# Interleaving the two projections with clustered attention, under one activation table set

## The chip, the cores and the metric

The kernel runs on one core of a Trainium2 chip. The metric is the device time of one execution in microseconds (us). A core has a matrix engine (TensorE, PE in the profile, with its weight loads as PEld), a vector engine (VectorE, DVE), an engine for activation functions (ScalarE, ACT), a general one (GpSimd, POOL) and an engine that here only issues transfers (SyncE, SP). Each works through its own queue in order and waits for others at semaphores.

## The reference

Attention over 4 batches, 8 heads, 768 positions of 64 values, in which a query sees only the keys of its own cluster, and then two projections with a gelu between them:

```python
q_assign = np.argmax(np.einsum('bhsd,hcd->bhsc', q_n, c_n), axis=-1)
k_assign = np.argmax(np.einsum('bhsd,hcd->bhsc', k_n, c_n), axis=-1)
mask = q_assign[:, :, :, None] == k_assign[:, :, None, :]
scores = np.where(mask, scale * np.matmul(q, k.transpose(0, 1, 3, 2)), -1000000000.0)
attn = softmax(scores)                       # over the keys
attn_out = np.matmul(attn, v)                # [4, 8, 768, 64]
x = attn_out.transpose(0, 2, 1, 3).reshape(3072, 512)
out = gelu(x @ w_in) @ w_out                 # w_in [512, 2048], w_out [2048, 512]
```

There are 16 cluster centroids per head. The function returns float32 [3072, 512].

## The kernel before, in words

Two stages follow each other.

The attention stage runs over 32 heads (4 batches of 8). The loop over `t` (line 260) is a software pipeline written out by hand: while head `t` has its scores, exps and value products, head `t+1` gets its one-hot cluster rows and head `t+2` its transposes and cluster dots. The 768 positions are 6 chunks of 128.

- Preparing a head: q and k are split into a bf16 part and its remainder (lines 128 to 132, VectorE), transposed on TensorE (line 152), copied to `q_stack` and `k_stack` (line 156), multiplied with the centroids (line 163), reduced to one-hot rows of the nearest centroid (lines 171 to 180, VectorE), which are transposed too (line 187) and copied under the 64 data rows (lines 192 and 194). So one product of 80 rows gives the score plus a large bonus where the clusters agree.
- Scores: for each key chunk a tile `e_ps` of 128 keys by 768 queries (line 202, as 512 and 256 columns; two such tiles in PSUM). ScalarE takes its exp with scale and bias into `e_sb` (line 211).
- Value products: `v_sb` of a chunk carries 64 columns of values and 64 of ones, so the product with `e_sb` (line 219) gives numerators in rows 0 to 63 of `av_ps` and the sum of exps in rows 64 to 127. `av_ps` is one tile of 768 columns, accumulated over the 6 chunks.
- Closing a head: VectorE copies the numerators (line 229), ScalarE takes the logarithm of the denominators straight from `av_ps` (line 230), then exp(-log) as the reciprocal (line 237), and VectorE writes their product to `xT` in bf16 (line 240).

The projection stage runs over 6 blocks of 512 tokens: 16 tiles of `x @ w_in` (line 333, 4 matmuls of 512 columns each, four PSUM tiles), each followed by a gelu (line 338), and then 4 output tiles (line 343, 16 matmuls of 512 columns each, four PSUM tiles), copied by VectorE and ScalarE in turn (lines 350 and 352) and stored (line 359).

In the code, the transposes and dots of head `t+2` are "fills", handed out between the chunks by `emit_fills`. Tile pools say how many buffers each tile has, and a scheduler sets the final order of each engine's queue from the program order and the dependences. The activation functions come from table sets; a load is put in wherever the next function isn't in the set that is active.

Of the kernel before, what the change touches and what calls it, by code (L numbers as in the profile page):

```python
# [18 lines left out]
def kernel(  # L19
# [22 lines left out]
    SCALE = 1.0 / float(D) ** 0.5  # L42
    SPLITS = [(0, 512), (512, 256)]
# [11 lines left out]
    cent_sq = consts.tile([H * NCL, 1], FP32)  # L55
    cent_scr = consts.tile([H * NCL, D], FP32)
    nc.scalar.activation(cent_scr, cent_sb, ACT.Square, accum_out=cent_sq)
    cent_norm = consts.tile([H * NCL, 1], FP32)
    nc.scalar.sqrt(cent_norm, cent_sq)
    cent_rnorm = consts.tile([H * NCL, 1], FP32)  # L60
    nc.vector.reciprocal(cent_rnorm, cent_norm)
    cent_n = consts.tile([H * NCL, D], FP32)
# [3 lines left out]
    with tc.tile_pool(name="ps_init", bufs=1, space=bass.MemoryType.PSUM) as ps_init:  # L66
# [6 lines left out]
            out=cn_big[0:D, :, :, 1],  # L73
# [4 lines left out]
    w_in_sb = consts.tile([P, DM // P, DF], BF16)  # L78
    w_out_sb = consts.tile([P, DF // P, DM], BF16)
# [14 lines left out]
    xT = xt_pool.tile([P, DM // P, NTOK], BF16)  # L94

    NIT = B * H
    NV = 4

    with tc.tile_pool(name="qk", bufs=3) as qk_pool, \
# [3 lines left out]
         tc.tile_pool(name="rcp", bufs=2) as rcp_pool, \  # L103
         tc.tile_pool(name="ps_stk", bufs=1, space=bass.MemoryType.PSUM) as ps_stk_pool, \
         tc.tile_pool(name="ps_e", bufs=2, space=bass.MemoryType.PSUM) as ps_e_pool, \
         tc.tile_pool(name="ps_av", bufs=1, space=bass.MemoryType.PSUM) as ps_av_pool:

        st = {}

        def st_dma_qk(i):  # L110
            b, h = divmod(i, H)
            s = st.setdefault(i, {})
            s["q_sb"] = qk_pool.tile([P, NCH, D], FP32, name="q_sb")
            s["k_sb"] = qk_pool.tile([P, NCH, D], FP32, name="k_sb")
            nc.sync.dma_start(out=s["q_sb"], in_=q[b, h].rearrange("(p x) d -> p x d", p=P))
            nc.sync.dma_start(out=s["k_sb"], in_=k[b, h].rearrange("(p x) d -> p x d", p=P))

        def st_dma_v(i):
            b, h = divmod(i, H)
            nc.gpsimd.dma_start(  # L120
                out=v_sb[:, i % NV, :, 0:D],
                in_=v[b, h].rearrange("(p x) d -> p x d", p=P))
# [85 lines left out]

        def st_exp(i, j):
            s = st[i]  # L210
            nc.scalar.activation(s["e_sb"][:, j, :], s["e_ps_j"], ACT.Exp,  # L211
                                 bias=ebias, scale=SCALE)

        def st_av(i, j):
            s = st[i]
            if j == 0:
                s["av_ps"] = ps_av_pool.tile([P, S], FP32, name="av_ps")
            for (c0, cw) in SPLITS:
                nc.tensor.matmul(  # L219
                    s["av_ps"][:, c0:c0 + cw],  # L220
                    v_sb[:, i % NV, j, :],
                    s["e_sb"][:, j, c0:c0 + cw],
                    start=(j == 0), stop=(j == NCH - 1))

        def st_avrelease(i):
            s = st[i]
            num = rcp_pool.tile([D, S], FP32, name="num")
            lnden = rcp_pool.tile([D, S], FP32, name="lnden")
            nc.vector.tensor_copy(num, s["av_ps"][0:D, :])  # L229
            nc.scalar.activation(lnden, s["av_ps"][D:2 * D, :], ACT.Ln)  # L230
            s["num"], s["lnden"] = num, lnden

        def st_norm(i):
            b, h = divmod(i, H)
            s = st[i]
            recip = rcp_pool.tile([D, S], FP32, name="recip")
            nc.scalar.activation(recip, s["lnden"], ACT.Exp, scale=-1.0)  # L237
            col = (h % 2) * D
            chunk = h // 2
            nc.vector.tensor_tensor(  # L240
                out=xT[col:col + D, chunk, b * S:(b + 1) * S],
                in0=s["num"], in1=recip, op=ALU.mult)
            del st[i]

        st_dma_qk(0), st_dma_qk(1), st_dma_qk(2)
        st_dma_v(0), st_dma_v(1)
# [13 lines left out]
        for t in range(NIT):  # L260
            if t + 3 < NIT:
                st_dma_qk(t + 3)
            if t + 2 < NIT:
                st_dma_v(t + 2)
            if t + 2 < NIT:
                st_hilo(t + 2)

            st_qk(t, 0)
            st_exp(t, 0)
            st_qk(t, 1)  # L270
            st_exp(t, 1)

            if t + 1 < NIT:
                st_ohT(t + 1)
                st_scatter(t + 1)

            p2 = t + 2 < NIT
            if p2:
                st_alloc_ps(t + 2)

            fills = []
            if p2:
                fills += [("T", "q", j) for j in range(NCH)]
                fills += [("SC", "q", None)]
                fills += [("T", "k", j) for j in range(NCH)]
                fills += [("SC", "k", None)]
                fills += [("D", "q", j) for j in range(NCH)]
                fills += [("D", "k", j) for j in range(NCH)]
            per_chunk = [0, 2, 6, 8, 10, 10]

            fi = 0

            def emit_fills(n):
                nonlocal fi
                cnt = 0
                while fi < len(fills) and cnt < n:
                    kind, side, j = fills[fi]
                    if kind == "T":
                        st_transpose(t + 2, side, j)
                    elif kind == "SC":  # L300
                        st_stackcopy(t + 2, side)
                        cnt -= 1
                    else:
                        st_dots(t + 2, side, j)
                    fi += 1
                    cnt += 1

            for j in range(NCH):
                emit_fills(per_chunk[j])
                st_av(t, j)  # L310
                if j + 2 < NCH:
                    st_qk(t, j + 2)
                    st_exp(t, j + 2)
            st_avrelease(t)
            emit_fills(10 ** 9)
            if p2:
                st_rowmax(t + 2)
            st_norm(t)

    TOKB = 512  # L320
    NTB = NTOK // TOKB

    with tc.tile_pool(name="moe_g", bufs=2) as moe_pool, \
         tc.tile_pool(name="moe_out", bufs=4) as out_pool, \
         tc.tile_pool(name="ps_h", bufs=4, space=bass.MemoryType.PSUM) as psum_h, \
         tc.tile_pool(name="ps_o", bufs=4, space=bass.MemoryType.PSUM) as psum_o:

        for tb in range(NTB):
            g_sb = moe_pool.tile([P, DF // P, TOKB], BF16, name="g_sb")
            for ft in range(DF // P):  # L330
                h_ps = psum_h.tile([P, TOKB], FP32, name="h_ps")
                for c in range(DM // P):
                    nc.tensor.matmul(  # L333
                        h_ps,
                        w_in_sb[:, c, ft * P:(ft + 1) * P],
                        xT[:, c, tb * TOKB:(tb + 1) * TOKB],
                        start=(c == 0), stop=(c == DM // P - 1))
                nc.scalar.activation(g_sb[:, ft, :], h_ps, ACT.Gelu)  # L338

            for tt in range(TOKB // P):  # L340
                o_ps = psum_o.tile([P, DM], FP32, name="o_ps")
                for ft in range(DF // P):
                    nc.tensor.matmul(  # L343
                        o_ps,
                        g_sb[:, ft, tt * P:(tt + 1) * P],
                        w_out_sb[:, ft, :],
                        start=(ft == 0), stop=(ft == DF // P - 1))
                o_sb = out_pool.tile([P, DM], FP32, name="o_sb")
                if tt % 2 == 0:
                    nc.vector.tensor_copy(o_sb, o_ps)  # L350
                else:
                    nc.scalar.copy(o_sb, o_ps)  # L352
                g0 = tb * TOKB + tt * P
                bb = g0 // S
                c0 = g0 % S
                x = c0 // P
                dst = out[bb * S:(bb + 1) * S].rearrange(
                    "(p x) m -> x p m", x=NCH)[x]
                nc.sync.dma_start(out=dst, in_=o_sb)


# [28 lines left out]
```

The softmax here doesn't subtract the row's maximum and nothing guards it: scores larger than these inputs give would overflow.

## Time and profile before

The median of five runs is 548.79 us (547.28 to 550.07); the profiled execution spans 547.0 us.

| group of the page | count | busy us | mean ns of one |
|---|---|---|---|
| exp of a score tile, line 211 (ACT) | 192 | 168.5 | 896 |
| table loads at lines 211 and 230 (ACT) | 64 | 82.2 | 1283 |
| logarithm, line 230, and reciprocal, line 237 (ACT) | 64 | 52.4 | 807, 830 |
| scores, line 202 (PE) | 384 | 122.9 | 399 |
| value products, line 219 (PE) | 384 | 120.8 | 413 |
| projections, lines 333 and 343 (PE) | 768 | 171.4 | 388, 379 |
| copy of the numerators, line 229 (DVE) | 32 | 30.3 | 948 |
| product with the reciprocal, line 240 (DVE) | 32 | 30.4 | 951 |

How to read it: busy time is the union of a group's executions, while the mean is of one execution with its latency. Matmuls overlap one another, so their busy time over their count is the price of one in a stream, and less than the mean. The page also shows TensorE's granted clock in tenths of full speed, in 40 slices of the span. A group's last column is the idle time of its engine just before it, with what ended most of that.

### The profile page before, as it was taken

What the parts mean: (1) busy time and instruction counts of PE and PEld (TensorE: products, weight loads), DVE (VectorE), ACT (ScalarE), POOL (GpSimd) and SP (SyncE); (2) the same over time, 40 slices, a digit from 0 to 9 for tenths busy, and PEclk for the clock granted to TensorE, in tenths of its full rate; (3) what the DMA queues carried; (4) which work ended last, traced back from release to release, by engine and by line L of the source; (5) the groups of instructions that cost most, each with busy time, mean ns of one, the idle gap of its engine ahead of it and who ended that gap; (6) DMA issues with size and microseconds to landing.
All of it is one profiled execution on the core that took longest, in us unless ns stands there. A gap on an engine that the chain in (4) does not pass through costs nothing.

```text
span 547.0 us, 6319 instructions
## 1 busy us (share of the span) xinstructions
PE 429.1 (78%) x2497; PEld 221.6 (41%) x2497; DVE 231.6 (42%) x532; ACT 369.0 (67%) x437; POOL 38.9 (7%) x63
## 2 busy tenths in 40 slices
PE   0367867977776777777677677677999999999997
PEld 0244433443443444344444343332444444444443
DVE  3675665565666666566656767421000000000000
ACT  2038898898889888888888999987434342425250
POOL 4330100100010010001000100000000000000000
PEclk9997797676788787778868989858899999999999
DMA  8992231232123223222322311000020102020201
GB/s 191 252 170 36 34 60 24 40 41 50 23 52 43 38 36 50 46 37 36 59 50 38 53 13 8 1 0 1 0 78 6 72 0 78 0 78 0 78 0 77
DMA packets 40813, 26.65 MB, mean 49 GB/s; under 512 B 26960, under 2 KB 37200, under 8 KB 40784
## 3 DMA queue, kind: packets, MB, share of 16 engines
q0 software_dynamic: 27968, 7.34, 13.4%
q1 hardware_dynamic: 12816, 18.91, 10.9%
q8 instruction: 19, 0.31, 0.2%
q14 instruction: 10, 0.08, 0.1%
HBM read 27.30 MB, written 6.29 MB: 61 GB/s over the span
## 4 chain that ended last, share of the span: by engine, by line
PE 55%; ACT 38%; DMA 3%; DVE 2%; issue 1%; SPq 0%; ACTq 0%
ACT e_sb L211 16%; PE h_ps L333 15%; PE o_ps L343 15%; PE av_ps L219 11%; PE e_ps L202 9%; ACT L230 8%; ACT L211 7%; ACT lnden L230 5%; DMA k_sb<-in_k_dram 3%; PE q_ps L152 2%; ACT recip L237 1%; PE k_ps L152 1%; PE q_ps L187 1%; ACT L338 1%; PE q_ps L163 1%
## 5 line engine op out<-in xcount | busy, mean ns | idle before, releaser
L211 ACT ACTIVATE e_sb<-e_ps,ebias 128x768 bf16<-128x768 f32 x192 | 168.5, 896 | 45.4 <-PE e_ps L202 42.1
L219 PE MATMUL av_ps<-e_sb,v_sb 128*128 128x512 bf16 (+1 forms) x384 | 120.8, 413 | 72.8 <-ACT lnden L230 38.5
L202 PE MATMUL e_ps<-q_stack,k_stack 80*128 80x512 bf16 (+1 forms) x384 | 122.9, 399 | 10.5 <-ACT e_sb L211 9.2
L333 PE MATMUL h_ps<-xT,w_in_sb 128*128 128x512 bf16 x384 | 87.2, 388 | 3.1 <-ACT g_sb L338 3.1
L343 PE MATMUL o_ps<-w_out_sb,g_sb 128*128 128x512 bf16 x384 | 84.2, 379 | 0.3 <-ACT lnden L230 0.3
L219 PEld LDWEIGHTS <-v_sb 128*128 128x128 bf16 x384 | 40.4, 111 | 99.8 <-issue 90.8
L338 ACT ACTIVATE g_sb<-h_ps 128x512 bf16<-128x512 f32 x96 | 56.9, 598 | 25.1 <-PE h_ps L333 25.0
L350 DVE COPY o_sb<-o_ps 128x512 f32<-128x512 f32 x12 | 8.3, 692 | 150.7 <-PE o_ps L343 150.7
L240 DVE TENSOR_TENSOR xT<-num,recip 64x768 bf16<-64x768 f32 x32 | 30.4, 951 | 87.2 <-ACT recip L237 87.2
L202 PEld LDWEIGHTS <-k_stack 80*128 80x128 bf16 x384 | 43.2, 116 | 43.9 <-issue 30.1
L333 PEld LDWEIGHTS <-w_in_sb 128*128 128x128 bf16 x384 | 38.3, 100 | 51.1 <-issue 7.8
L211 ACT ACT_TABLE_LOAD x32 | 41.1, 1283 | 24.9 <-PE e_ps L202 24.3
L352 ACT COPY o_sb<-o_ps 128x512 f32<-128x512 f32 x12 | 7.0, 586 | 74.3 <-PE o_ps L343 74.3
L343 PEld LDWEIGHTS <-g_sb 128*128 128x128 bf16 x384 | 37.6, 98 | 45.7 <-issue 0.6
L120 POOL DMA_DIRECT2D v_sb<-in_v_dram x32 | 26.2, 820 | 275.8 <-PE av_ps L219 255.9
L230 ACT ACT_TABLE_LOAD x32 | 41.1, 1283 | 0.6
L229 DVE COPY num<-av_ps 64x768 f32<-64x768 f32 x32 | 30.3, 948 | 17.9 <-PE av_ps L219 17.2
L152 PE MATMUL q_ps<-ident,q_hl 128*128 128x128 bf16 x192 | 24.7, 280 | 11.1 <-DVE cn_big L72 9.9
L152 PEld LDWEIGHTS <-q_hl 128*128 128x128 bf16 x192 | 19.5, 129 | 23.4 <-DVE cn_big L72 10.2
L152 PE MATMUL k_ps<-ident,k_hl 128*128 128x128 bf16 x192 | 26.5, 253 | 2.2 <-DVE dsum L172 2.2
L237 ACT ACTIVATE recip<-lnden 64x768 f32<-64x768 f32 x32 | 26.6, 830 | 0.0
L230 ACT ACTIVATE lnden<-av_ps 64x768 f32<-64x768 f32 x32 | 25.8, 807 | 0.4
(51 smaller groups left out, 305.1 us busy)
## 6 DMA issues: line engine op xcount, KB each, us to landing
q_sb<-in_q_dram SPq DMA_DIRECT2D x32, 192.0 KB, 2.4
k_sb<-in_k_dram SPq DMA_DIRECT2D x32, 192.0 KB, 2.4
out_dram<-o_sb SPq DMA_DIRECT2D x24, 256.0 KB, 2.0
v_sb<-in_v_dram POOLq DMA_DIRECT2D x32, 96.0 KB, 3.0
w_in_sb<-in_moe_w_in_dram POOLq DMA_DIRECT2D x4, 512.0 KB, 11.6
w_out_sb<-in_moe_w_out_dram POOLq DMA_DIRECT2D x16, 128.0 KB, 8.2
cent_sb<-in_centroids_dram SPq DMA_DIRECT2D x1, 32.0 KB, 1.8
```

The costliest lines, as they stand in the source:

```text
L120: nc.gpsimd.dma_start(out=v_sb[:, i % NV, :, 0:D], in_=v[b, h].rearrange("(p x) d -> p x d", p=P))
L152: nc.tensor.transpose(ps[:, j * P:(j + 1) * P], hl[:, j, :], ident)
L202: nc.tensor.matmul(e_ps[:, c0:c0 + cw], s["k_stack"][0:AUG, j * P:(j + 1) * P], s["q_stack"][0:AUG, c0:c0 + cw], start=True, stop=True)
L211: nc.scalar.activation(s["e_sb"][:, j, :], s["e_ps_j"], ACT.Exp, bias=ebias, scale=SCALE)
L219: nc.tensor.matmul(s["av_ps"][:, c0:c0 + cw], v_sb[:, i % NV, j, :], s["e_sb"][:, j, c0:c0 + cw], start=(j == 0), stop=(j == NCH - 1))
L229: nc.vector.tensor_copy(num, s["av_ps"][0:D, :])
L230: nc.scalar.activation(lnden, s["av_ps"][D:2 * D, :], ACT.Ln)
L237: nc.scalar.activation(recip, s["lnden"], ACT.Exp, scale=-1.0)
L240: nc.vector.tensor_tensor(out=xT[col:col + D, chunk, b * S:(b + 1) * S], in0=s["num"], in1=recip, op=ALU.mult)
L333: nc.tensor.matmul(h_ps, w_in_sb[:, c, ft * P:(ft + 1) * P], xT[:, c, tb * TOKB:(tb + 1) * TOKB], start=(c == 0), stop=(c == DM // P - 1))
L338: nc.scalar.activation(g_sb[:, ft, :], h_ps, ACT.Gelu)
L343: nc.tensor.matmul(o_ps, g_sb[:, ft, tt * P:(tt + 1) * P], w_out_sb[:, ft, :], start=(ft == 0), stop=(ft == DF // P - 1))
```

## The change

It has three parts that depend on each other.

1. One table set for exp and logarithm. A load of the set numbered 6, which holds both, is put into ScalarE's queue by hand: once after the square root of the setup, and again after the gelus of each projection block but the last. Exps are ordered after it without a semaphore, and the gelus after the last reciprocal before them.
2. PSUM room. The value products go through one bank of 512 columns in two passes: columns 0 to 511 along with the chunks as before, then 512 to 767 for all six chunks at once. VectorE copies numerators and denominators together to `nd` in SBUF after each pass, and ScalarE takes the logarithm from there. The bank that this frees holds an output tile of the down-projection (one buffer).
3. Projections inside the loop over heads. A batch's up-projection and gelus are called as one block, one head after the batch's last (after the last head, for the last batch), in tiles of 768 columns that use the score tiles' buffers. Its down-projection is cut into single matmuls and handed out between the chunks of the following heads: 2 after each chunk, 3 and 2 around the second pass. What is left goes before the next block, and after the loop for the last batch.

It is for taking most table loads off ScalarE, and for giving TensorE projection work while it would wait in the attention stage.

The diff, cut to its core:

```diff
+        load_ln_exp([sqrt_inst])
...
-                s["av_ps"] = ps_av_pool.tile([P, S], FP32, name="av_ps")
-            for (c0, cw) in SPLITS:
-                nc.tensor.matmul(
-                    s["av_ps"][:, c0:c0 + cw],
+                s["av_ps"] = ps_av_pool.tile([P, 512], FP32, name="av_ps")
+            nc.tensor.matmul(
+                s["av_ps"][:, 0:cw],
...
-            nc.vector.tensor_copy(num, s["av_ps"][0:D, :])
-            nc.scalar.activation(lnden, s["av_ps"][D:2 * D, :], ACT.Ln)
+            nc.vector.tensor_copy(s["nd"][:, c0:c0 + cw], s["av_ps"][:, 0:cw])
+            if pss == 1:
+                s["lnden"] = rcp_pool.tile([D, S], FP32, name="lnden")
+                nc.scalar.activation(s["lnden"], s["nd"][D:2 * D, :], ACT.Ln)
...
+        def emit_m1_block(bb):
+            g_sb = g_pool.tile([P, DF // P, S], BF16, name="g_sb")
+            for ft in range(DF // P):
+                h_ps = ps_e_pool.tile([P, S], FP32, name="e_ps")
+                for (c0, cw) in SPLITS:
+                    for c in range(DM // P):
+                        nc.tensor.matmul(
+                            h_ps[:, c0:c0 + cw],
+                            w_in_sb[:, c, ft * P:(ft + 1) * P],
+                            xT[:, c, bb * S + c0:bb * S + c0 + cw],
+                            start=(c == 0), stop=(c == DM // P - 1))
+                gelus.append(nc.scalar.activation(g_sb[:, ft, :], h_ps, ACT.Gelu))
+            for g in gelus:
+                after_inst(g, last_recip[0])
+            if bb < B - 1:
+                load_ln_exp(gelus)
...
+        def emit_m2(bb, x):
+            o_ps = ps_moe_pool.tile([P, DM], FP32, name="o_ps")
+            for ft in range(DF // P):
+                nc.tensor.matmul(
+                    o_ps, g_sb[:, ft, x * P:(x + 1) * P], w_out_sb[:, ft, :],
+                    start=(ft == 0), stop=(ft == DF // P - 1))
+                yield
...
             for j in range(NCH):
                 emit_fills(per_chunk[j])
-                st_av(t, j)
+                st_av(t, j, 0)
                 if j + 2 < NCH:
                     st_qk(t, j + 2)
                     st_exp(t, j + 2)
-            st_avrelease(t)
+                try_emit_m2(2)
+            st_avrelease(t, 0)
+            emit_fills(6)
+            try_emit_m2(3)
+            for j in range(NCH):
+                st_av(t, j, 1)
+            st_avrelease(t, 1)
+            try_emit_m2(2)
             emit_fills(10 ** 9)
             if p2:
                 st_rowmax(t + 2)
             st_norm(t)
...
+            if (t % H == 0 and t > 0) or t == NIT - 1:
+                bb = t // H if t == NIT - 1 else t // H - 1
+                try_emit_m2(10 ** 9)
+                emit_m1_block(bb)
+                m2_queue.extend((bb, x) for x in range(NCH))
+
+        try_emit_m2(10 ** 9)
```

More of the change, by code (lines that the diff above doesn't have):

```diff
@@ L58 @@
     cent_norm = consts.tile([H * NCL, 1], FP32)
-    nc.scalar.sqrt(cent_norm, cent_sq)
+    sqrt_inst = nc.scalar.sqrt(cent_norm, cent_sq)
     cent_rnorm = consts.tile([H * NCL, 1], FP32)
@@ L105, with after_inst, load_ln_exp @@
          tc.tile_pool(name="ps_e", bufs=2, space=bass.MemoryType.PSUM) as ps_e_pool, \
-         tc.tile_pool(name="ps_av", bufs=1, space=bass.MemoryType.PSUM) as ps_av_pool:
+         tc.tile_pool(name="ps_av", bufs=1, space=bass.MemoryType.PSUM) as ps_av_pool, \
+         tc.tile_pool(name="ps_moe", bufs=1, space=bass.MemoryType.PSUM) as ps_moe_pool, \
+         tc.tile_pool(name="moe_g", bufs=1) as g_pool, \
+         tc.tile_pool(name="moe_out", bufs=3) as out_pool:
         st = {}
+        set_load = [None]
+        def after_inst(inst, prev):
+            tc.add_manual_dep(inst.ins, prev.ins.name, mybir.DependencyInfo(
+                mybir.DependencyClass.NoSync, mybir.DependencyReason.DATA), reason="set order")
+        def load_ln_exp(prev):
+            inst = nc.scalar.add_instruction(mybir.InstLoadActFuncSet(
+                name=nc.get_next_instruction_name(), act_func_set_id=6))
+            for p in prev:
+                after_inst(inst, p)
+            set_load[0] = inst
+        load_ln_exp([sqrt_inst])
         def st_dma_qk(i):
@@ L210, in st_exp, with st_av, st_avrelease @@
             s = st[i]
-            nc.scalar.activation(s["e_sb"][:, j, :], s["e_ps_j"], ACT.Exp,
-                                 bias=ebias, scale=SCALE)
-        def st_av(i, j):
+            inst = nc.scalar.activation(s["e_sb"][:, j, :], s["e_ps_j"], ACT.Exp,
+                                        bias=ebias, scale=SCALE)
+            after_inst(inst, set_load[0])
+        def st_av(i, j, pss):
             s = st[i]
+            c0, cw = SPLITS[pss]
             if j == 0:
-                s["av_ps"] = ps_av_pool.tile([P, S], FP32, name="av_ps")
-            for (c0, cw) in SPLITS:
-                nc.tensor.matmul(
-                    s["av_ps"][:, c0:c0 + cw],
[L221 to L225, printed above, removed]
-            s = st[i]
-            num = rcp_pool.tile([D, S], FP32, name="num")
-            lnden = rcp_pool.tile([D, S], FP32, name="lnden")
-            nc.vector.tensor_copy(num, s["av_ps"][0:D, :])
-            nc.scalar.activation(lnden, s["av_ps"][D:2 * D, :], ACT.Ln)
-            s["num"], s["lnden"] = num, lnden
+                s["av_ps"] = ps_av_pool.tile([P, 512], FP32, name="av_ps")
+            nc.tensor.matmul(
+                s["av_ps"][:, 0:cw],
+                v_sb[:, i % NV, j, :],
+                s["e_sb"][:, j, c0:c0 + cw],
+                start=(j == 0), stop=(j == NCH - 1))
+        def st_avrelease(i, pss):
+            s = st[i]
+            c0, cw = SPLITS[pss]
+            if pss == 0:
+                s["nd"] = rcp_pool.tile([P, S], FP32, name="nd")
+                s["num"] = s["nd"][0:D]
+            nc.vector.tensor_copy(s["nd"][:, c0:c0 + cw], s["av_ps"][:, 0:cw])
+            if pss == 1:
+                s["lnden"] = rcp_pool.tile([D, S], FP32, name="lnden")
+                nc.scalar.activation(s["lnden"], s["nd"][D:2 * D, :], ACT.Ln)
         def st_norm(i):
@@ L236, in st_norm @@
             recip = rcp_pool.tile([D, S], FP32, name="recip")
-            nc.scalar.activation(recip, s["lnden"], ACT.Exp, scale=-1.0)
+            last_recip[0] = nc.scalar.activation(recip, s["lnden"], ACT.Exp, scale=-1.0)
             col = (h % 2) * D
@@ L243, in st_norm, with try_emit_m2 @@
             del st[i]
+        gst = {}
+        last_recip = [None]
+        m2_queue = []
+        m2_flip = [0]
+        def emit_m1_block(bb):
+            g_sb = g_pool.tile([P, DF // P, S], BF16, name="g_sb")
+            gst[bb] = g_sb
+            gelus = []
+            for ft in range(DF // P):
[13 more added lines that the diff above has]
+        def emit_m2(bb, x):
+            g_sb = gst[bb]
+            o_ps = ps_moe_pool.tile([P, DM], FP32, name="o_ps")
[4 more added lines that the diff above has]
+                yield
+            o_sb = out_pool.tile([P, DM], FP32, name="o_sb")
+            if m2_flip[0] % 2 == 0:
+                nc.vector.tensor_copy(o_sb, o_ps)
+            else:
+                nc.scalar.copy(o_sb, o_ps)
+            m2_flip[0] += 1
+            dst = out[bb * S:(bb + 1) * S].rearrange("(p x) m -> x p m", x=NCH)[x]
+            nc.sync.dma_start(out=dst, in_=o_sb)
+        m2_now = [None]
+        def try_emit_m2(n):
+            while n > 0:
+                if m2_now[0] is None:
+                    if not m2_queue:
+                        return
+                    m2_now[0] = emit_m2(*m2_queue.pop(0))
+                try:
+                    next(m2_now[0])
+                    n -= 1
+                except StopIteration:
+                    m2_now[0] = None
         st_dma_qk(0), st_dma_qk(1), st_dma_qk(2)
@@ L318 @@
             st_norm(t)
[L320 to L359, printed above, removed]
+            if (t % H == 0 and t > 0) or t == NIT - 1:
[4 more added lines that the diff above has]
+        try_emit_m2(10 ** 9)
 _INS = ['q', 'k', 'v', 'centroids', 'moe_w_in', 'moe_w_out']
```

## The prediction

> **What bounds the kernel now.** I read the totals and the slices of the page first, to see whether one engine holds the whole span.
>
> ```profile
> PE 429.1 (78%) x2497; PEld 221.6 (41%) x2497; DVE 231.6 (42%) x532; ACT 369.0 (67%) x437; POOL 38.9 (7%) x63
> PE   0367867977776777777677677677999999999997
> DVE  3675665565666666566656767421000000000000
> ACT  2038898898889888888888999987434342425250
> PEclk9997797676788787778868989858899999999999
> ```
>
> No engine does: there are two stages. Up to slice 27 (about 370 us) ScalarE shows eights and nines, TensorE sixes and sevens at a lowered clock; after it TensorE shows nines, ScalarE half of that and VectorE nothing. A table by stage puts numbers on it (busy time of each engine, then the granted clock).
>
> ```profile
> core 0: us, PE busy (x) PEld busy (x) DVE busy (x) ACT busy (x) POOL busy (x), PEclk, DMA share, GB/s
> 200.00:290.00 90.00, 67.61 (x442) 38.68 (x441) 55.95 (x128) 75.89 (x82) 6.54 (x8) 0.77 0.26 42
> 400.00:540.00 140.00, 140.00 (x650) 63.49 (x649) 7.32 (x11) 53.62 (x90) 0.00 (x0) 1.00 0.10 40
> ```
>
> In the attention stage ScalarE is busy 84% of the time. In the projections TensorE is busy throughout: 650 matmuls of 512 columns in 140 us is 0.215 us each, 0.227 over the whole stage (lines 333 and 343: 171.4 us over 768). I take 0.227. The groups by line tell what ScalarE does, and the timeline of one head shows the order (start, length, what; in brackets the idle time before).
>
> ```profile
> L211 ACT ACTIVATE e_sb<-e_ps,ebias 128x768 bf16<-128x768 f32 x192 | 168.5, 896 | 45.4 <-PE e_ps L202 42.1
> L219 PE MATMUL av_ps<-e_sb,v_sb 128*128 128x512 bf16 (+1 forms) x384 | 120.8, 413 | 72.8 <-ACT lnden L230 38.5
> L211 ACT ACT_TABLE_LOAD x32 | 41.1, 1283 | 24.9 <-PE e_ps L202 24.3
> L230 ACT ACT_TABLE_LOAD x32 | 41.1, 1283 | 0.6
> ```
>
> ```profile
> 216.60 1.28 ACT L230 ACT_TABLE_LOAD   x1
> 217.89 0.81 ACT L230 ACTIVATE lnden<-av_ps 64x768 f32<-64x768 f32 x1
> 218.72 1.28 ACT L211 ACT_TABLE_LOAD   x1
> 218.75 0.81 PE L219 MATMUL av_ps<-e_sb,v_sb 128*128 128x512 bf16 x4 [1.08 <-ACT lnden L230]
> 220.01 0.90 ACT L211 ACTIVATE e_sb<-e_ps,ebias 128x768 bf16<-128x768 f32 x1
> 220.96 0.49 PE L219 MATMUL av_ps<-e_sb,v_sb 128*128 128x512 bf16 x2 [1.34 <-ACT e_sb L211]
> ```
>
> Each head pays two table loads of 1.28 us around its logarithm, and TensorE waits for both: the next head's first value product waits for the logarithm to free the accumulator, then for an exp behind the second load. These waits sum to 38.5 us plus part of the 33.5 us on exps. They also lower the clock: it is 1.00 at 217.07 to 222.19, when TensorE idles, and 0.50 from 223.90, when the head's matmuls come. Then exps wait for scores (42.1 us).
>
> **What the skill says.** "ScalarE: Activation LUTs", section "Table sets: the hidden batching unit": exp and ln have a set in common, so ln then exp costs one load. The trace agrees that the present sets don't hold both: 64 loads for 32 heads. Its section "What ACT_TABLE_LOAD costs" gives 1283 ns, the trace's mean, and some 1380 ns of drain; the trace shows no such gap (the logarithm starts 0.01 us after its load), so I price a load at 1.28. "TensorE: Matmul & The Clock Gate", Part 1, says that a spell of activity of about 3.4 us raises the clock to full and an idle one halves it. The trace shows only 0.50 and 1.00 as levels, in step with that; it doesn't say how busy is enough.
>
> **Part 1, one table set.** The built program has 10 table loads where there were 70: 3 in the setup, then a gelu load for each of 4 projection blocks and 3 loads back. 60 x 1.28 = 77 us leave ScalarE, nearly all from the attention stage, where they lie on the path. What is left per head is 6 exps at 0.88 (168.5/192), 0.81 and 0.83: 6.9 us. The first load also moves ahead of the first scores, 1.3 us earlier (exp at 28.8 us where the load stood).
>
> **Part 2, value products in two passes.** The accumulator shrinks to one bank of 512 columns, used twice per head, and is freed by VectorE alone. The matmul columns stay. VectorE's copy of 768 columns (949 ns) becomes one of 512 (692 ns, from the output copy of that shape) and one of 256: the slope (949-692)/256 is 1.0 ns per column, so 435 ns. Together 1.13, or 0.18 more per head. New wait: the second pass stands behind the first copy, with scores, one-hot transposes and projection matmuls around it. The built order on TensorE puts two score tiles of the next head ahead of the second pass, so ScalarE has some 1.8 us of exps at hand; I cost that wait at nothing for ScalarE and leave VectorE's 0.18.
>
> VectorE then becomes a limit: 55.95 us over 8 heads is 7.0, plus 0.18, plus half the output copies (3 x 0.69 per 8 heads, 0.26) is 7.2 to 7.4 us per head, above ScalarE's 6.9.
>
> **Part 3, down-projection as filler.** TensorE per head at full clock: scores and products 12 x (0.227 + 0.114) = 4.1; 18 transposes at 0.083 (six take 0.50) = 1.5; 12 small dots at 0.05 (six take 0.30) = 0.6. Sum 6.2 us; measured, 67.6/8 = 8.5 at clock 0.77 is 6.5, so it fits. A batch's down-projection is 96 matmuls, 17 per head by the calls (12 + 3 + 2), so 5.6 heads carry 17 x 0.227 = 3.9 us more each: 10.1 us, and TensorE is their bound. The rest of the heads are bound by VectorE.
>
> **Part 4, up-projection blocks.** 16 tiles x 4 x (0.227 + 0.114) = 21.8 us of TensorE; a gelu of 768 columns (about 0.9, as the exp of that shape) hides under the next tile's 1.36. Entry: copy 0.69, second pass 0.7, copy 0.43, logarithm 0.81, recip 0.83, load 1.28, first gelu 0.9 is 5.6 us, against two up-projection tiles (2.7) and transposes. The rest overlaps the head's own slack: from 0 to 3 us, I take 1. Exit: load and first exp, 2.2 us, against 11 filler matmuls (2.5) in the built order: nothing. Two more orders are added: gelus stand behind the last recip, which costs only the entry just counted, and the single gelu buffer makes a block wait for the former batch's down-projection, done 2.4 heads before. Block: 22.8.
>
> **Part 5, tail.** The last batch's six output tiles have nothing beside them: 96 x 0.227 = 21.8. The single output bank makes five tiles wait for the copy before, 0.64 plus about 0.3 of handover: 4.7. After the last copy starts, 3.9 us as now (543.09 to 547.0). Sum 30.4.
>
> **The sum.** Coupled engines with single buffers don't reach their busiest one: 7.25 at 85% is 8.5 us for a head without filler (bounds 7.4 and 10.2, see below), and 10.1 at 95% is 10.6 with. Heads 0 to 8 carry none: 9 x 8.5 = 76.5. Batches 1 and 2: 5.6 x 10.6 + 2.4 x 8.5 = 79.8 each. The last 7 heads: 59.4 + 1.4 x 8.5 = 71.3. So 28.8 + 76.5 + 4 x 22.8 + 2 x 79.8 + 71.3 + 30.4 = 457.8. The last two heads prepare no successors and fall towards ScalarE's 6.9, some 1.6 us less each; the last head's closing chain (copy, logarithm, recip, product) has nothing beside it, up to 4 us. These about cancel; I round down to 455 us.
>
> **Rivals.** *Tighter.* Heads at VectorE's 7.4, filler heads at 10.1, blocks at 21.8: 28.8 + 66.6 + 87.2 + 2 x (56.6 + 17.8) + (56.6 + 10.4) + 30.4 = 429. For it: the order was laid with next scores ahead. Against: VectorE's own queue waits 22.1 us per 90 at the last product (line 240).
>
> *Cold clock.* TensorE in heads without filler is at 6.2 of 8.5, 73% busy. If that doesn't hold full clock, they run as now at about 0.77: 6.2/0.75 = 8.3 plus the present slack of 2 gives 10.2 us. 9 + 2.4 + 2.4 + 1.4 = 15.2 heads lose 1.7: 26 us; the 17 filler heads lose perhaps 0.5: 8. So 489. For it: the present slices of 0.50. Against: the stall that precedes each is what goes, and the long spells of full work show 1.00.
>
> *Slower.* If the wait for the copy took the place of the loads, heads stayed at 10.7 us ((372 - 30)/32) and nothing were hidden, the 547 would gain 24 handovers of the output bank at 1 us and four entries at 6: 595. Against: the ten loads left can't fill that idle time, and TensorE's idle 22 us per 90 is real room.
>
> **How the numbers follow.** Forecast 0.6, tighter 0.15, cold clock 0.21, slower 0.04, of which 0.01 for no change. The bounds of the head (7.4 to 10.2) make 429 to 489; I leave a little beyond the cold end, as its filler loss is a guess, and cut the tight end where it stands: 428 to 490.
>
> **What would show it.** After: ten loads; heads 0 to 8 at 8 to 9 us with clock above 0.9; filler heads at 10 to 11 with TensorE over 90% busy; ScalarE idle about 20% in attention with its waits on scores; VectorE over 80% busy in heads without filler. A clock of 0.75 there shows the cold rival; waits of value products on copies longer than 1 us per head would refute Part 2; blocks over 26 us, Part 4.

## The result, and the profile after

The changed kernel takes 428.08 us (median of 9 runs, 425.58 to 429.97) against 548.36 (16 runs): a ratio of 0.7802, 95% interval 0.7782 to 0.7822. That is 120 us less, where 94 were forecast: the point of 455 is 27 us too high, and the time sits on the lower edge of the range, where the "tighter" rival (429) had it.

The totals and slices of the page after (40 slices of 10.6 us):

```profile
span 425.0 us, 6527 instructions
...
PE 367.3 (86%) x2625; PEld 207.8 (49%) x2625; DVE 233.0 (55%) x564; ACT 284.9 (67%) x345; POOL 39.2 (9%) x63
...
PE   0077989897999999987999999997999999779985
...
DVE  2386899899105787798007777895017655200000
ACT  4012999997579767895687687877697787766200
...
PEclk9999999999999999999999999999999999989999
```

The two stages are gone: TensorE shows sevens to nines from slice 3 to 39, and its clock drops only once in this profile, for 3.4 us where the last projection block begins. It does the same products as before (in 2625 matmuls in place of 2497, as the up-projection is cut finer) in 367 us of busy time in place of 429, since they hardly run at half clock any more (mean clock 0.996 in place of 0.869). ScalarE has lost 84 us (369.0 to 284.9). The groups that answer to those of before:

```profile
L230 ACT ACTIVATE e_sb<-e_ps,ebias 128x768 bf16<-128x768 f32 x192 | 165.8, 895 | 44.8 <-PE e_ps L221 43.5
...
L239 PE MATMUL av_ps<-e_sb,v_sb 128*128 128x256 bf16 (+1 forms) x384 | 95.8, 328 | 12.2 <-ACT e_sb L230 10.4
...
L254 ACT ACTIVATE lnden<-nd 64x768 f32<-64x768 f32 x32 | 26.9, 842 | 25.2 <-DVE nd L251 24.7
```

The exps cost what they did (895 ns each), and the 44.8 us of idle time before them is now for the larger part the start of the kernel (23.6 us until the first score, in one wait). TensorE's idle time before value products fell from 72.8 to 12.2 us. New are 24.7 us in which the logarithm waits for VectorE's copy to `nd`; they lie at the entries of the blocks and in heads with filler, and none in the first seven heads after head 0. The groups of 32 table loads at the exp and at the logarithm have no successors. ScalarE's timeline in a head without filler (start, length, what) shows it:

```profile
67.37 0.84 ACT L254 ACTIVATE lnden<-nd 64x768 f32<-64x768 f32 x1
68.23 0.90 ACT L230 ACTIVATE e_sb<-e_ps,ebias 128x768 bf16<-128x768 f32 x1
69.03 0.83 ACT L260 ACTIVATE recip<-lnden 64x768 f32<-64x768 f32 x1
69.77 3.37 ACT L230 ACTIVATE e_sb<-e_ps,ebias 128x768 bf16<-128x768 f32 x4
```

Logarithm, exp, reciprocal and four exps follow each other without a gap. Last, the table by stage, cut at the first exp and where ScalarE starts the reciprocal of head 0 and those of heads 8, 16, 24 and 31, which a projection block follows (heads count from 0; columns as in the prediction):

```profile
0.00:29.40 29.40, 6.55 (x58) 4.88 (x59) 13.83 (x40) 4.40 (x6) 12.66 (x31) 1.00 1.01 216
29.40:48.61 19.21, 15.33 (x110) 8.28 (x109) 14.04 (x39) 10.42 (x12) 4.18 (x6) 1.00 0.76 111
48.61:102.66 54.05, 47.26 (x412) 28.38 (x412) 50.97 (x128) 48.78 (x60) 6.55 (x8) 1.00 0.38 65
102.66:194.80 92.14, 88.59 (x651) 50.57 (x649) 56.57 (x136) 70.50 (x86) 6.70 (x8) 1.00 0.30 61
194.80:287.62 92.82, 88.67 (x658) 50.78 (x658) 57.57 (x140) 70.47 (x85) 6.69 (x8) 1.00 0.29 58
287.62:372.82 85.20, 78.38 (x527) 43.14 (x527) 36.99 (x83) 63.53 (x77) 2.45 (x3) 1.00 0.13 24
372.82:425.00 52.18, 42.55 (x218) 21.75 (x217) 3.03 (x4) 16.84 (x21) 0.00 (x0) 0.97 0.08 30
```

The first row is the start, the second head 0, the third heads 1 to 8. Then come two cycles, each a projection block and 8 heads, a shorter cycle of a block and 7 heads, and the last block with the tail.

### The profile page after: what moved, and what is told of

It is laid out like the page before. It is cut to its first block, busy times and chain, and to the rows that moved or that the text cites. A ratio compares the mean times of both kernels' runs of the same rounds, so it can differ in the third digit from the quotient of the medians.

```text
span 425.0 us, 6527 instructions
## 1 busy us (share of the span) xinstructions
PE 367.3 (86%) x2625; PEld 207.8 (49%) x2625; DVE 233.0 (55%) x564; ACT 284.9 (67%) x345; POOL 39.2 (9%) x63
## 4 chain that ended last, share of the span: by engine, by line
PE 61%; ACT 19%; DVE 14%; DMA 4%; issue 1%; SPq 1%; DVEq 0%
PE e_ps L281 18%; PE o_ps L296 16%; PE av_ps L239 11%; ACT e_sb L230 10%; PE e_ps L221 10%; ACT lnden L254 4%; DMA k_sb<-in_k_dram 4%; ACT recip L260 3%; DVE nd L251 3%; PE q_ps L206 2%; DVE xT L263 2%; PE k_ps L171 2%; DVE k_stack L175 1%; DVE k_hl L151 1%; PE q_ps L171 1%
## 5 line engine op out<-in xcount | busy, mean ns | idle before, releaser
L230 ACT ACTIVATE e_sb<-e_ps,ebias 128x768 bf16<-128x768 f32 x192 | 165.8, 895 | 44.8 <-PE e_ps L221 43.5
L296 PE MATMUL o_ps<-w_out_sb,g_sb 128*128 128x512 bf16 x384 | 105.2, 379 | 3.9 <-DVE o_sb L302 2.4
L239 PE MATMUL av_ps<-e_sb,v_sb 128*128 128x256 bf16 (+1 forms) x384 | 95.8, 328 | 12.2 <-ACT e_sb L230 10.4
L221 PE MATMUL e_ps<-q_stack,k_stack 80*128 80x512 bf16 (+1 forms) x384 | 96.3, 332 | 0.6
L281 PE MATMUL e_ps<-xT,w_in_sb 128*128 128x512 bf16 (+1 forms) x512 | 87.1, 329 | 3.3 <-DVE xT L263 3.2
L286 ACT ACTIVATE g_sb<-e_ps 128x768 bf16<-128x768 f32 x64 | 51.5, 810 | 30.9 <-PE e_ps L281 30.9
L254 ACT ACTIVATE lnden<-nd 64x768 f32<-64x768 f32 x32 | 26.9, 842 | 25.2 <-DVE nd L251 24.7
L251 DVE COPY nd<-av_ps 128x512 f32<-128x512 f32 x64 | 35.5, 554 | 13.6 <-PE av_ps L239 13.0
L263 DVE TENSOR_TENSOR xT<-nd,recip 64x768 bf16<-64x768 f32 x32 | 30.4, 950 | 11.2 <-ACT recip L260 10.4
L175 DVE COPY k_stack<-k_ps 128x768 bf16<-128x768 bf16 x32 | 17.7, 553 | 28.3 <-PE e_ps L221 24.6
L171 PEld LDWEIGHTS <-q_hl 128*128 128x128 bf16 x192 | 14.1, 101 | 22.2 <-DVE cn_big L72 10.1
L175 DVE COPY q_stack<-q_ps 128x768 bf16<-128x768 bf16 x32 | 17.8, 556 | 8.7 <-PE q_ps L171 7.2
```

What stands on the lines that cost most here:

```text
L171: nc.tensor.transpose(ps[:, j * P:(j + 1) * P], hl[:, j, :], ident)
L221: nc.tensor.matmul(e_ps[:, c0:c0 + cw], s["k_stack"][0:AUG, j * P:(j + 1) * P], s["q_stack"][0:AUG, c0:c0 + cw], start=True, stop=True)
L230: inst = nc.scalar.activation(s["e_sb"][:, j, :], s["e_ps_j"], ACT.Exp, bias=ebias, scale=SCALE)
L239: nc.tensor.matmul(s["av_ps"][:, 0:cw], v_sb[:, i % NV, j, :], s["e_sb"][:, j, c0:c0 + cw], start=(j == 0), stop=(j == NCH - 1))
L251: nc.vector.tensor_copy(s["nd"][:, c0:c0 + cw], s["av_ps"][:, 0:cw])
L254: nc.scalar.activation(s["lnden"], s["nd"][D:2 * D, :], ACT.Ln)
```

## The experiments

Theory A: each head takes the time of its busiest engine, and what held the old heads at 10.7 us was the table loads; the interleaving is then hidden only up to what TensorE has free in a head. Theory B: it is the interleaved projection work that brings the time, by filling TensorE and so holding its clock up.

### The table set alone

The kernel before, with only the common set loaded by hand and the gelus ordered after the last reciprocal:

```diff
+        load_ln_exp([sqrt_inst])
...
+            after_inst(inst, set_load[0])              # each exp
...
-                nc.scalar.activation(g_sb[:, ft, :], h_ps, ACT.Gelu)
+                after_inst(nc.scalar.activation(g_sb[:, ft, :], h_ps, ACT.Gelu), last_recip[0])
```

> The kernel before with one edit: the common table set for exp and logarithm, loaded by hand once, and the gelus ordered after the last reciprocal. Theory A (each head runs at the rate of its busiest engine, 7.0 us without filler; table loads were what held heads at 10.7): first reciprocal at about 49, 31 more heads at 7.0 to 7.5, then 172 + 4 of projections: 442 to 457 us, clock of TensorE near 1 in the heads. So the set alone gives 75 to 90% of the gain of 120 us. Theory B (TensorE is slow between its waits because it goes to half clock, and only the filler keeps it at full clock): heads stay at 9 to 10 us, 500 to 530 us, clock near 0.75 in the heads.

Measured: 430.24 us, ratio 0.7852 (0.7823 to 0.7881), better than either theory had it: heads take 6.85 us on average where theory A had 7.0 to 7.5, and 169 us follow the last reciprocal where it had 176. Totals, ScalarE's slices and the clock from its page:

```profile
PE 371.7 (87%) x2455; PEld 197.0 (46%) x2497; DVE 228.0 (53%) x532; ACT 282.3 (66%) x371; POOL 39.1 (9%) x63
...
ACT  4012999999999999999999997327144162350620
...
PEclk9999999999999999999999999999999999999999
```

A stage of eight heads in it, reciprocal to reciprocal:

```profile
101.53:156.53 55.00, 49.68 (x428) 30.48 (x433) 52.05 (x124) 53.40 (x65) 6.57 (x8) 1.00 0.40 66
```

Eight heads in 55.00 us are 6.87 us each, with ScalarE busy 53.40 of it (97%) and TensorE's clock at 1.00, with no filler at all. Nearly the whole gain is in this one part of the change, which thus depends on neither of the others; theory B falls as an account of the gain. ScalarE runs a head in the order that it had before (five exps, the logarithm, an exp, the reciprocal), only without the loads.

### The set and the two passes, projections after the loop

The changed kernel with its projections put back behind the loop, as before:

```diff
-            if (t % H == 0 and t > 0) or t == NIT - 1:
-                bb = t // H if t == NIT - 1 else t // H - 1
-                try_emit_m2(10 ** 9)
-                emit_m1_block(bb)
-                m2_queue.extend((bb, x) for x in range(NCH))
-        try_emit_m2(10 ** 9)
+    for tb in range(NTB):                              # the stage of the kernel before
...
```

> The changed kernel with its set and its two passes of the value products, but with both projections after the loop as in the kernel before. Theory A: heads at 7.0, projections 172 after them: 49 + 31 x 7.0 + 176 = 442 us; the interleaving is then worth only about 14 us of the 120. Against the run with the set alone: the same to 15 us faster if the logarithm that holds the accumulator was a wait there, 6 us slower if the two passes cost VectorE 0.18 us a head. Theory B: over 480 us, since without filler the clock falls.

Measured: 436.11 us, ratio 0.796 (0.7921 to 0.7999). So the two passes cost 5.9 us, the second of the two expectations: from first to last reciprocal 31 heads take 216.15 us against 212.25, 0.13 more each (0.18 was worked out for VectorE), and the first reciprocal comes 0.9 later. Sixteen heads of it:

```profile
102.65:215.47 112.82, 98.89 (x852) 58.53 (x866) 108.77 (x273) 105.36 (x130) 13.14 (x16) 1.00 0.42 69
```

They take 7.05 us each, with VectorE busy 96% and ScalarE 93% of it, so with two passes VectorE is the limit of a head without filler. Interleaving then takes 8.0 us off. Together the second and third parts of the change bring some 2 us, hardly outside the intervals.

### Interleaving without the set

The changed kernel without its hand-placed loads, so that the two sets alternate:

```diff
-        load_ln_exp([sqrt_inst])
...
-            after_inst(inst, set_load[0])
...
-            if bb < B - 1:
-                load_ln_exp(gelus)
```

> The changed kernel without its hand-placed loads, so that the two sets alternate again, with two passes and interleaved projections kept. Theory A: ScalarE's head is 6.6 + 2.6 = 9.2 us of work in a row with waits of its own, so heads with and without filler take about 10 to 10.7; 15 heads lose 3.5 and 17 lose 1.5: 428 + 52 + 26 = about 505 us (495 to 520). Theory B: the filler holds the clock up and the time stays under 460.

Measured: 520.17 us, ratio 0.9493 (0.9444 to 0.9543), 15 above theory A's figure and just past the upper end of its range. Heads 1 to 8, without filler, and then two heads that carry filler:

```profile
50.55:129.98 79.43, 58.86 (x409) 34.54 (x415) 52.47 (x126) 69.45 (x76) 6.58 (x8) 0.81 0.27 45
177.76:200.41 22.65, 19.44 (x142) 10.70 (x144) 14.74 (x35) 19.80 (x23) 1.64 (x2) 1.00 0.32 68
```

The first eight take 9.93 us each, ScalarE is busy 87% and the clock is at 0.81, much as in the kernel before. The two with filler run at full clock, as theory B has it, and still take 11.3 us each, with ScalarE busy 87% again: a full clock doesn't take the loads away. Against the kernel before this one is 27 us faster, while the second and third parts bring 2 us under the common set. What they are worth thus depends on the loads, and the gains of the parts don't add up.

### Loads put back, two and one per head

The kernel with the set alone, with loads of the very set that is active already put around the logarithm; the second kernel has only the first of the two:

```diff
+            ld1 = nc.scalar.add_instruction(mybir.InstLoadActFuncSet(..., act_func_set_id=6))
+            after_inst(ld1, s["last_exp"])
             ln = nc.scalar.activation(lnden, s["av_ps"][D:2 * D, :], ACT.Ln)
+            after_inst(ln, ld1)
+            ld2 = nc.scalar.add_instruction(mybir.InstLoadActFuncSet(..., act_func_set_id=6))
+            after_inst(ld2, ln)
...
+            after_inst(last_recip[0], s["ld2"])
```

> The kernel with the set alone (430 us), with two loads of that same set put back per head, one before and one after the logarithm, so that nothing but ScalarE's time changes (64 loads, 82 us). Theory A: ScalarE's head becomes 6.6 + 2.6 = 9.2 us in a row; if nothing else follows, 430 + 31 x 2.35 = 503 us. If the stalls also drop TensorE's clock, as in the kernel before, exps wait for scores and it comes to 530 to 550 with a clock near 0.8 in the heads. If it was the change of set and not the load that cost, 430 to 440.

> The kernel with the set alone and one load of the same set put back per head, before the logarithm (32 loads, 41 us). If a load costs just its own time on ScalarE's queue: 430 + 31 x 1.28 = 470 us. If the cost grows once the stalls are long enough to halve TensorE's clock: nearer 450 with one load, since half the stall is half of little. Two loads cost 112 us, 3.6 a head; half of that would be 486.

Measured: 542.38 us with two (ratio 0.991, 0.9886 to 0.9935) and 477.77 with one (0.8698, 0.8648 to 0.8748). The loads before the logarithm in the kernel with two (the group after it has the same busy time and mean):

```profile
L247 ACT ACT_TABLE_LOAD x32 | 41.1, 1283 | 0.6
```

Two neighbouring heads of it in the table by stage, and the start of the second:

```profile
214.69:224.42 9.73, 6.93 (x54) 3.71 (x54) 6.90 (x17) 9.40 (x10) 0.82 (x1) 1.00 0.29 51
224.42:235.18 10.76, 8.12 (x54) 4.28 (x54) 7.14 (x17) 9.52 (x10) 0.82 (x1) 0.84 0.28 47
225.00:229.40 4.40, 3.66 (x17) 1.87 (x18) 2.81 (x6) 3.26 (x5) 0.00 (x0) 0.61 0.24 57
```

The loads change no set, and with two of them 112 of the 118 us came back: it is the load that costs and not the change of set. With one load 47.5 us came back, 8 more than its own time was expected to cost. That is 3.6 and 1.5 us per head, where the loads themselves are 2.57 and 1.28. The two kernels are not the one with the set alone plus ScalarE's time and nothing else, though: under the new dependences the scheduler ordered the queues anew (an exp stands between the first load and the logarithm, for instance).

The rows show where the rest comes from. The first head runs at full clock throughout and takes 9.73 us, close to ScalarE's own 9.40. The second has a spell of half clock in its first matmuls (0.61 over the 4.4 us of the third row) and takes 10.76. All heads of the two kernels divide like this. With two loads, 11 heads at full clock take 9.73 us and the 20 others 10.35 to 11.58; with one, 23 at full clock take 8.08 and the 8 others, the last one aside, 8.88 to 9.34. The kernel before itself has two heads at full clock; one of them (head 27), and after it a usual one (head 12):

```profile
326.73:336.11 9.38, 6.77 (x60) 4.06 (x60) 6.58 (x16) 9.17 (x11) 0.82 (x1) 1.00 0.16 10
167.62:177.97 10.35, 7.58 (x55) 4.49 (x55) 6.75 (x16) 9.28 (x11) 0.82 (x1) 0.84 0.25 38
```

At full clock a head with its two loads takes 9.38 us, 2.5 more than the 6.87 without them; the average of heads 1 to 31 is 10.64. So the stall costs twice: by estimate some 77 us of the 118 by itself (31 heads at 2.5), and some 40 again in heads in which TensorE runs in part at half clock. No run changed the clock alone, so this rests on comparing heads of the same kernel, and why the clock falls in some heads and not in others is not shown. The Trainium skill, "ScalarE: Activation LUTs", section "What ACT_TABLE_LOAD costs", puts a switch of sets at 2.66 us with its drain. The two switches in a head of the kernel before cost 2.5 us together at full clock, so the trace shows no drain.

### More work for VectorE or ScalarE

To see which engine sets a head without loads, one operation more per head, into a tile nobody reads. First on VectorE, in the changed kernel and in the kernel with the set alone; then on ScalarE in the latter:

```diff
+            nc.vector.tensor_tensor(out=scr, in0=s["q_sb"], in1=s["k_sb"], op=ALU.subtract)
```

```diff
+            nc.scalar.copy(scr, s["q_sb"])
```

> The changed kernel with one more VectorE subtraction of 128x384 (0.55 us) in each head, into a tile that nobody reads. Theory A (VectorE is at its limit in heads without filler, TensorE in the others): 15 heads x 0.55 = 8 us slower, 436 us, all of it in the heads without filler. If ScalarE alone sets the heads without filler: under 2 us. If VectorE lies on the path of all heads: 17 us, 445 us.

> The kernel with the set alone and one more VectorE subtraction of 0.55 us in each head, into a tile nobody reads. In its heads of 6.85 us VectorE is busy 6.20 and ScalarE 6.56. If the busiest engine sets the head: 6.20 + 0.55 = 6.75, still under 6.85, so 430 to 434 us. If VectorE lies on the path of each head: 430 + 17 = 447.

> The kernel with the set alone and one more ScalarE copy of 128x384 (about 0.5 us) in each head, into a tile nobody reads. If the busiest engine sets the head: 6.56 + 0.5 = 7.06 plus the present 0.3 of gaps, 31 x 0.5 = 15 us, 445. If VectorE or TensorE set the heads: under 8 us.

Measured: 433.95 us (0.7929, 0.7884 to 0.7973), 438.22 (0.7983, 0.7954 to 0.8011) and 434.70 (0.7925, 0.7889 to 0.7962). The first is 6 above the changed kernel, where 8 were expected, but not in the expected place: in its profile seven heads without filler take 7.11 us each in place of 6.97 (VectorE busy 47.50 of 49.74 us), 0.9 us in all, while the three cycles are longer by 5.5. The added operations don't fall evenly, one to a head: of the 32, nine run before the first reciprocal and four in these seven heads. So this run says little on what sets which head. The other two missed their figures in opposite directions, and they too have nine of the 32 before the first reciprocal. The kernel with the set alone and more VectorE work, heads 1 to 14 and then 15 to 28:

```profile
48.63:143.38 94.75, 85.15 (x725) 50.10 (x723) 89.49 (x210) 91.22 (x113) 11.47 (x14) 1.00 0.38 60
143.38:247.93 104.55, 87.74 (x758) 50.15 (x756) 100.78 (x240) 92.45 (x113) 10.64 (x13) 1.00 0.34 59
```

And fourteen heads of the one with more ScalarE work:

```profile
103.99:203.22 99.23, 90.63 (x758) 52.98 (x756) 94.27 (x225) 96.90 (x127) 11.54 (x14) 1.00 0.41 71
```

With more VectorE work the first 14 heads take 6.77 us each and ScalarE is the busier engine (96%): they hold 8 of the added operations and VectorE splits q and k for only 11 heads in them, so it lives on a lead from the start. In the next 14 it has 15 of them, a head takes 7.47 us and VectorE is busy 96% of it. With more ScalarE work a head takes 7.09, and ScalarE is busy 98%. So in each stretch the head lasts about as long as its busiest engine works. This is read from the stretches afterwards: by the totals as expected, 434.70 would have spoken for another engine than ScalarE, and 438.22 lies between the two cases.

The expectations took wrong bases. VectorE's 6.20 was a mean that counts the last heads, which prepare no successors: the eight heads shown above have 52.05/8 = 6.5 us. On ScalarE the copy lengthened the work in a row by only 0.24 us (6.92 against 6.68 per head), since operations that stand end to end overlap in the records (the eight of a head without the copy sum to 7.01 us by their means and cover 6.68).

### Filler spread thinner, and a tail with two buffers

The changed kernel with 1 down-projection matmul after each chunk in place of 2; with the last batch's output tiles in the score tiles' two buffers; and with both:

```diff
-                try_emit_m2(2)
+                try_emit_m2(1)
             st_avrelease(t, 0)
```

```diff
+            if bb == B - 1:
+                o_ps = ps_e_pool.tile([P, S], FP32, name="e_ps")[:, 0:DM]
+            else:
+                o_ps = ps_moe_pool.tile([P, DM], FP32, name="o_ps")
-            o_ps = ps_moe_pool.tile([P, DM], FP32, name="o_ps")
```

> The changed kernel with the down-projection spread thinner: 1 matmul after each chunk in place of 2, so 11 per head in place of 17, and all 8 heads carry some in place of 5. Theory A (each head takes the time of its busiest engine, so filler is hidden only up to the 1.2 us that TensorE has free in a head of 7.0): heads of 5.7 + 11 x 0.215 = 8.1 us, 8 of them 65 us, against 44.7 for five and 21 for three now; two full cycles and a shorter one save about 3 each at best, 419 us (417 to 423). If the filler costs by its waits and not by its amount: within 2 us of 428.

> The changed kernel with one edit: the last batch's six output tiles alternate between the two score tiles' buffers in place of the single output bank. Theory A: the five handovers of 0.67 to 0.84 us in the tail go, 3.7 us, 424.4 us. If the tail is held by something else (weights, stores): under 1 us.

> Both edits of the two runs before in one kernel. Theory A: they lie in different stretches and add up: about 415 us, faster than the kernel with the set alone (430) by 15. If thinner filler brings nothing: 424.

Measured: 418.14 us (0.7634, 0.7616 to 0.7651), 424.85 (0.7741, 0.771 to 0.7772) and 413.03 (0.7538, 0.7526 to 0.7551), the totals as theory A had them; the second varied most, from 420.9 to 428.25 over six runs. First the changed kernel's heads without filler (seven of them) and with it (five):

```profile
48.61:97.43 48.82, 42.38 (x366) 25.22 (x366) 46.07 (x114) 46.32 (x57) 5.73 (x7) 1.00 0.41 68
136.44:181.11 44.67, 44.25 (x342) 25.00 (x341) 34.56 (x84) 34.04 (x43) 4.10 (x5) 1.00 0.37 80
```

Without filler TensorE is busy 87% of 6.97 us, so a head has some 0.9 to 1.2 us free. The heads with filler carry 15 matmuls each, 3.2 us at 0.215, and are 8.93 us long with TensorE 99% busy: 8.93 - 6.97 = 1.96 us of the 3.2, some 60%, lengthens the head. Five heads carry nearly all of it, and the others have room they don't use. Spread out, in the same stretch:

```profile
137.29:185.03 47.74, 46.56 (x355) 25.74 (x361) 39.11 (x95) 38.58 (x48) 4.93 (x6) 1.00 0.39 76
```

six heads take 7.96 us each. The two full cycles fall from 92.1 and 92.8 us to 90.2 and 90.7, and the shorter one from 85.2 to 80.1. The sum is the expected one, but its share is not 3 for each: the shorter cycle gains most, as its last two heads, which prepare no successors, take 28 matmuls in place of 7 and get no longer.

The tail of the changed kernel in TensorE's timeline:

```profile
395.57 3.62 PE L296 MATMUL o_ps<-w_out_sb,g_sb 128*128 128x512 bf16 x16
399.97 3.61 PE L296 MATMUL o_ps<-w_out_sb,g_sb 128*128 128x512 bf16 x16 [0.78 <-DVE o_sb L302]
404.26 3.61 PE L296 MATMUL o_ps<-w_out_sb,g_sb 128*128 128x512 bf16 x16 [0.67 <-ACT o_sb L304]
...
417.39 3.61 PE L296 MATMUL o_ps<-w_out_sb,g_sb 128*128 128x512 bf16 x16 [0.84 <-DVE o_sb L302]
```

And of the one with two buffers:

```profile
394.25 20.88 PE L299 MATMUL e_ps<-w_out_sb,g_sb 128*128 128x512 bf16 x94
```

Each of the five later tiles waits 0.67 to 0.84 us for the copy of the one before, 3.7 us in all. With two buffers the six tiles are one block of 20.88 us without a wait. The kernel with both edits beats the changed one by 15 us.

## Why the prediction was right and where it was wrong

Right: the direction, the table loads as what bounded the kernel, ten loads left, the clock back at full, filler heads bound by TensorE, VectorE as the limit of the others (96% busy in the sixteen heads of the kernel with two passes), the blocks and the tail. The sum, term by term, against the stages of the trace:

| term | forecast us | measured us |
|---|---|---|
| start to the first exp | 28.8 | 29.4 |
| heads 0 to 8 | 76.5 | 73.3 |
| cycle of batch 1 (block and 8 heads) | 102.6 | 92.1 |
| cycle of batch 2 | 102.6 | 92.8 |
| cycle of batch 3 (block and 7 heads) | 94.1 | 85.2 |
| last block and tail | 53.2 | 52.2 |
| sum (455 after rounding) | 457.8 | 425.0 |

29 of the 33 us are in the three cycles, so in the heads. The mechanism was right and two sizes were off.

*Heads without filler: forecast 8.5, measured 6.97.* "Coupled engines with single buffers don't reach their busiest one: 7.25 at 85%" is the step that failed, twice over. The larger error is the 85%, a judgement without a row behind it: in every kernel here without loads in its heads the busiest engine reaches 95 to 98% of the head (95% ScalarE and 94% VectorE in the changed one). At 95% the same 7.25 gives 7.6 us, so this makes 0.9 of the 1.5. The rest is the base: VectorE's 7.25 rested on "over 8 heads", while by the reciprocals of the trace that window of 90 us holds 8.2, which makes 55.95/8.2 = 6.8; measured, with the second copy, it is 46.07/7 = 6.58, and 108.77/16 = 6.80 in the sixteen heads with two passes. In heads 0 to 8 this hid behind a term left out of the sum: head 0 takes 19.2 us from first exp to reciprocal, not 8.5, while its successors are still being prepared. The two errors cancel there by luck and show fully in the cycles.

*Heads with filler: forecast 10.6, measured 8.93.* Four small terms go the same way: under filler TensorE's base is (44.25 - 75 x 0.215)/5 = 5.6 us in place of 6.2; a matmul costs 0.215 in place of 0.227 (the average over the old projection stage still held its first part, with the clock at 0.91 from 380 to 400 us); a head carries 15 and not 17, since 22 or 23 of a batch's 96 start before these five heads; and TensorE reached 99%, not 95%.

*Part 1* was sized at 77 us, with the waits and the clock counted nowhere in that figure. The runs show this part alone worth 118 us: some 77 are the stall itself, and the rest goes with heads that ran in part at half clock. It didn't enter the total wrongly, since the total was built up from the new heads, but the text left open which part of the change brings the time, and it reads as though the filler were needed. It isn't: 430.2 without.

*Part 2*: the 0.18 us per head was about right (0.13), and the value products wait only 0.5 us in all for the copies. The wait that was put at nothing for ScalarE is there, 24.7 us at the logarithm, but in block entries and in heads that TensorE bounds. The part is a net loss of 6 us that pays for the bank of part 3.

*Part 3*: hidden by some 40% only, as the heads themselves already use TensorE to 87%. *Part 4*: blocks of about 22 us (from reciprocal to last gelu 22.2), as forecast. *Part 5*: right to 1 us, handovers included.

The tighter rival's 429 is met in part by luck: it had heads 0 to 8 at 66.6 us (measured 73.3) and the full cycles at 96.2 (92.1 and 92.8), errors that cancel. The cold rival fell: 73% was forecast as TensorE's share without filler and it came out at 87%, with the clock at 1.00. Whether 73% would have held full clock stays open: with two loads put back, heads with TensorE 71% busy did in 11 cases of 31. The slower rival did not come about.

Not settled: what makes the clock fall in one head with loads and not in the next, and what the two projections would gain with the value accumulator in one pass as well: the change takes its output bank from there, and it wasn't tried.

## What to carry to other kernels

Price a stall on the busiest engine with what it does to the engines behind it: here two table loads cost a head 2.5 us where the clock held and 3.8 on average, and taking them off alone gave 118 of 120 us. Work moved under another stage is hidden only as far as its engine is free there; count that per unit (0.9 to 1.2 us a head), and spread the work to fit before adding buffers or passes to make room for it. And don't put a factor like the 85% on a term that enters the sum over 30 times without a measured stretch behind it: it cost about 1 us per head here.

## What the runs showed of the hardware

A load of the set that is already active is not skipped: 64 of them took 1283 ns each, as those that change the set. The share of a head in which TensorE is busy doesn't by itself decide its clock: it stayed at 1.00 with 87% busy (the changed kernel), with 84 to 91% in the kernels with the set alone, and with 71% in 11 heads of the kernel with two loads, while the 20 others of that kernel ran in part at half clock. Three engines ran at 87, 94 and 95% of the same 48.8 us with one PSUM buffer for all tiles but the scores.
